# Preparing two more chunks of a Mish MLP without TensorE transposes, in a fused long-convolution and MLP kernel

## The chip, the cores and the metric

The kernel runs on one core of one Trainium2 chip. The metric is the device time of one execution in microseconds (us). Three runs of the kernel before gave 358.87 us as the median (358.83 to 359.21).

## The reference, cut to what matters

There are S = 2048 positions of D = 448 channels, and an inner width F = 1792. One sum of three terms is computed from q, k, v and x:

```python
xn = layernorm(q)                                  # per position, over D
kv = shift_conv4(k) * v                            # 4-tap causal convolution, per channel
y  = irfft(rfft(kv, 2S) * rfft(ssm_k, 2S))[:S] + kv * ssm_D
h  = xn @ w1 + b1
out = q + xn * y + mish(h) @ w2                    # mish(h) = h * tanh(softplus(h))
```

## The kernel before

**The MLP.** The 2048 positions are cut into 8 chunks of 256 (two halves, jj = 0 and 1, of 128). A chunk goes through 7 pairs of F tiles, so there are 56 pairs, and the work is written out in slots: slot 2i is GEMM 1 of pair i (22 matmuls of 256 columns, L512), slot 2i+1 holds the Mish of pair i (ScalarE, L520), its split into a high and a low part (a cast on ScalarE, a subtraction on VectorE, L84 and L85) and GEMM 2 of pair i-2 (12 matmuls of 448 columns, L544 to L546). Chunk c owns slots 14c to 14c+13. Both GEMMs are made of products of high and low parts, to keep float32 precision. When a chunk's last pair is through, its PSUM is added to q and so evicted (g2_evac, L551) on VectorE, at slot 2(7c+9): slot 18 for chunk 0, slot 32 for chunk 1. The store of the result is issued on SyncE one slot later (g2_out, L557), except for the last two chunks.

**The convolution** runs between. A "visit" is one group of matmuls (f1_mm, L146) of the first FFT step, over two row blocks: 8 visits of the filter h, at the slots of H_AT (L26), and 8 of kv, at those of KV_AT (L27: 24, 29, 34, 39, 44, 50, 55, 59). Below, h5 or k1 is the load of that visit's tensor (h_load L132, k_load L172, v_load L176). Before a kv visit, VectorE makes the four taps (taps, L189 to L202); the third tap's product is made on GpSimd (taps_pool, L182), started by a memset on VectorE (L181) that stands directly ahead of a fold. Behind a visit comes the fold (f1_fold): ScalarE copies one PSUM half to SBUF (L152), VectorE adds and subtracts (L156). Both write the tile `st`, of which there are two in turn; f1_out stores it to DRAM (L167), for kv from ScalarE's queue three slots after the visit. From slot 66 on, the later FFT steps follow.

**Getting x into GEMM 1.** GEMM 1 needs the normalised chunk with channels on partitions, as XH (high) and XL (low). There are two ways, and NT (4 before) is the first chunk that takes the second.

- Chunks 0 to 3: q is loaded with positions on partitions (ln_load, L390), its mean and spread are taken (bn_stats L406, bn_aggr L409, eps L412 on VectorE, the power on GpSimd L415), GpSimd subtracts and multiplies (norm, L419; tail, L423), TensorE transposes four 128x128 blocks for each half into a PSUM tile of GEMM 1's pool (L464), and the result is copied to XH (ScalarE, L476) and subtracted to XL (VectorE, L474). For chunk 2 this stands at slots 14 to 26, for chunk 3 at 28 to 40.
- Chunks 4 to 7: the host hands in q transposed as well, and xT_load (L434, 512 KB) reads a chunk of it into the one tile XN. The same statistics are taken; mean and reciprocal spread are stored to a small DRAM tile MR by a GpSimd DMA (nt_store, L442); nt_row (L445) reads them back for one half, broadcast to all 128 partitions, into `idr`; nt_norm (L451) subtracts and multiplies with that row, two VectorE operations over 512 elements for each half; nt_split copies to XH (ScalarE, L458) and subtracts to XL (VectorE, L459).

`idr` lies over the identity matrix that the transposes use, and there is one of it: the row of the second half waits until the first half is normalised.

**Order.** Nothing is reordered: each engine executes its instructions in program order, and each DMA is issued from the queue of its engine, in its order, after the waits it carries. `at(slot, ...)` puts work ahead of a slot's Mish and matmuls, `after(slot, ...)` behind them. Small VectorE steps of the statistics go into a list, `drip`, one of which is issued at each `dv()`; "flush" issues what is left. The slots for chunks from NT on are given relative to a base, b:

```python
NT_AT = {"q": -5, "x": -1, "stats": -2, "flush": 0, "row": (4, 8), "norm": (7, 10), "split": (8, 11)}
NT_SOON = dict(NT_AT, row=(4, 5), norm=(4, 7), split=(6, 8))
```

The weights w1 and w2 are loaded and split into high and low parts in the first 15 slots (w2_split, L84 and L85); w2's pair 5 is split behind slot 13 and used in slot 15.

Of the kernel before, what the change touches and what calls it, by code (L numbers as in the profile page):

```python
# [17 lines left out]
NP = NF // 2  # L18
CH = 256
NCHUNK = S // CH  # L20
NO = 8
EPS = 1e-5

G2_LAG = 2
# [5 lines left out]
I2_AT = {100: ((6, 7, 0, 1), 92, (95, 97, 98, 99), (0, 2, 0, 1)),  # L30
         108: ((2, 3, 4, 5), 101, (104, 105, 106, 107), (0, 1, 0, 1))}
LATE = 2
NT = 4
NT_AT = {"q": -5, "x": -1, "stats": -2, "flush": 0, "row": (4, 8), "norm": (7, 10), "split": (8, 11)}
NT_SOON = dict(NT_AT, row=(4, 5), norm=(4, 7), split=(6, 8))
NT_HOW = {c: NT_SOON for c in (3, 4, 7)}
NT_HOW[5] = dict(NT_AT, q=-8, stats=-4, flush=-2)
WARM_N = (448, 448, 448)
FILL_N = (224, 112, 96)
# [3 lines left out]
def tile_kernel(ctx: ExitStack, tc, q, qT, k, v, sk, hT, sD, w10, w1, w2, c_fib, c_g, c_gi, c_i2, out):  # L43
    nc = tc.nc
    V = nc.vector
# [17 lines left out]
    Dkv = dp.tile([NO * 16, 32, D], F32, name="Dkv")  # L63
    E = dp.tile([NJ * 4, 64, D], F32, name="E")
    MR = {c: dp.tile([2, CH], F32, name="MR") for c in range(NT, NCHUNK)}

# [8 lines left out]
    def rs(c):  # L75
        return rstd[:, 2 * c:2 * c + 2] if c < NT else mv[:, 2 * c:2 * c + 2, 1]

# [26 lines left out]
    def dv(n=1):  # L104
        for _ in range(n):
            if drip:
                drip.pop(0)()
# [4 lines left out]
    def at(slot, fn, *args):  # L112
        plan.setdefault(int(slot), []).append((fn, args))

    def after(slot, fn, *args):
        plan2.setdefault(int(slot), []).append((fn, args))
# [278 lines left out]
    def xn_tile():  # L395
        return mp.tile([128, 4, CH], F32, name="xn", bufs=1)

    def ln_parts(c):
        st = mp.tile([128, 2, 6], F32, name="bst", bufs=2)
        ve = mp.tile([128, 2], F32, name="ve", bufs=2)  # L400
        if c < NT:
            XN[c] = xn = xn_tile().rearrange("p a b -> p (a b)").rearrange("p (j d) -> p j d", j=2)
        eng = nc.gpsimd if 0 < c < NCHUNK - 1 else V

        def stats(jj):
            V.bn_stats(st[:, jj], Q[c][:, jj])  # L406

        def aggr(jj):
            V.bn_aggr(mv[:, 2 * c + jj], st[:, jj])  # L409

        def eps(a, b):
            V.tensor_scalar(ve[:, a:b], mv[:, 2 * c + a:2 * c + b, 1], EPS, None, op0=ALU.add)  # L412

        def power(a, b):
            nc.gpsimd.tensor_tensor(rs(c)[:, a:b], ve[:, a:b], mhalf[:, a:b], op=ALU.pow)  # L415

        def norm(jj):
            j = 2 * c + jj
            eng.tensor_scalar(xn[:, jj, :D], Q[c][:, jj], mv[:, j, 0:1], rs(c)[:, jj:jj + 1],  # L419
                              op0=ALU.subtract, op1=ALU.mult)  # L420

        def tail(a, b, copy=eng.tensor_copy):
            copy(xn[:, a:b, D:], xn[:, a:b, D - 64:D])  # L423

        return stats, aggr, eps, power, norm, tail, ve
# [21 lines left out]
    def nt_norm(c, jj):  # L447
        x = XN[c][:, :, 128 * jj:128 * jj + 128]
        for t, op in enumerate((ALU.subtract, ALU.mult)):
            m = idr.rearrange("p (a t) -> p t a", t=2)[:, t:t + 1].to_broadcast([128, 4, 128])  # L450
            V.tensor_tensor(x, x, m, op=op)  # L451
            dv()

    def nt_split(c, jj):
        if jj == 0:
# [22 lines left out]
    def ln_T(c, jj):  # L478
        if jj == 0:
            dv(len(drip))  # L480
            x_tiles(c)
        p = pg()
        transposes(c, jj, p)
        for lo in range(2):
            x_split(c, jj, p, lo)
# [73 lines left out]
    def mlp_slot(s):  # L559
# [3 lines left out]
        if half == 0:  # L563
            if i < n:
                c, p = pairs[i]
                if c + 1 < NT:
                    if p == 0:
# [8 lines left out]
        else:  # L576
            if i < n:
                c, p = pairs[i]
                if p == NP - 2 and c + 1 < NT:
                    ln_T(c + 1, 0)  # L580
# [27 lines left out]
    for g, t in enumerate(KV_AT):  # L608
        d = t - (KV_AT[g - 1] if g else t - 6)
        at(t - d - (3 if g > 1 else 2), k_load, g)  # L610
        at(t - d - 1, v_load, g)
        for u in range(4):
            after(t - (2 if g else 1) - d + d * u / 4, taps, g, u)
        at(t, f1_mm, KV, g, "kv")
        if g + 1 < NO:
            after(t, taps_pool, g + 1, 2)
        after(t, f1_fold, g, "kv")
        at(t + (3 if g < NO - 1 else 2), f1_out, Dkv, g, "kv")

    for p in range(NP):  # L620
        if p >= 3:
            at(max(2 * p - 5, 0), w1_load, p)
        if p == 1 or p > 2:
            at(2 * p - 2, w1_split, p)
        p and at(2 * p + (1 if p < 5 else 0), w2_load, p)
        at(2, w2_split, p) if p == 0 else after(2 * (p + G2_LAG) - 1, w2_split, p)

    at(OCT_AT[0], regroup)
    for o in range(NO):
# [34 lines left out]

    for c in range(NT, NCHUNK):
        at_ = NT_HOW.get(c, NT_AT)
        b = 2 * NP * (c - 1) + (1 if c == NT else 0)
        at(b + at_["q"], ln_load, c)
        at(b + at_["x"], xT_load, c)
        at(b + at_["stats"], nt_stats, c)  # L670
        at(b + at_["flush"], lambda: dv(len(drip)))
        for jj in range(2):
            at(b + at_["row"][jj], nt_row, c, jj)
            after(b + at_["norm"][jj], nt_norm, c, jj)
            after(b + at_["split"][jj], nt_split, c, jj)
# [28 lines left out]
    stats, aggr, eps, power, norm, tail, ve = ln_parts(0)  # L704
# [120 lines left out]
```

## Time and profile before

| what | value |
|---|---|
| median of three runs | 358.87 us |
| the profiled execution's own time | 359.38 us |
| its span in the trace | 357.6 us |
| busy time of TensorE (PE) | 352.0 us |
| busy time of VectorE (DVE) | 269.1 us |
| busy time of ScalarE (ACT) | 156.8 us |
| busy time of GpSimd (POOL) | 76.5 us |
| transposes, L464, 32 of them | 5.0 us |
| GpSimd's normalising, L419, 6 of them | 15.8 us |

The profile is of one execution. Its span runs from the first to the last instruction; the execution's own time is 1.8 us longer. PE is TensorE's matmul, PEld its weight load, and a Q behind an engine's name (SPq, ACTq) is that engine's queue of DMA issues. A row of a timeline gives the start, the duration, the engine, the line, the operation and what it writes and reads, and in square brackets the idle time ahead of it and what ended it. A row of the chain of waits gives the start, the time that it holds in the chain, the engine, the tile and the line. A row of waits gives who waited for whom: us in all, times, longest. Durations of neighbouring rows on TensorE overlap, since matmuls are pipelined, so 5.0 us of transposes is not 5.0 us of the span.

### The profile page before, as it was taken

Reading aid. Unit: us, or ns where it says so; the run is one execution under the profiler, and the core shown is the slowest. Engines: PE = TensorE matmul, PEld = TensorE weight load, DVE = VectorE, ACT = ScalarE, POOL = GpSimd, SP = SyncE. Lnnn points to the kernel's source line nnn. Section 1 sums busy time; section 2 is a strip of 40 time slices with the busy share of each in tenths; the row PEclk is TensorE's granted clock in tenths of the full one; section 3 lists DMA queues with packets and bytes.
Section 4 is the critical chain, followed back from the end, with each engine's and each line's share of the span. In section 5 each row is a group of like instructions: output and inputs, shape, how many; then the busy total and the mean of one; then the engine's idle time right before and its main releaser. Section 6 shows DMA issues by size and latency. Waiting matters only on the chain.

```text
span 357.6 us, 7445 instructions
## 1 busy us (share of the span) xinstructions
PE 352.0 (98%) x3100; PEld 290.2 (81%) x3100; DVE 269.1 (75%) x371; ACT 156.8 (44%) x267; POOL 76.5 (21%) x81
## 2 busy tenths in 40 slices
PE   8999999999999999999999999999999999999995
PEld 2988888888888989889997758767775699979795
DVE  5999568999999899899537757756863933788942
ACT  3976643344241542342333453455445343354480
POOL 2037001920128240213000030011031116040030
PEclk9999999999999999999999999999999999999999
DMA  7999978849586446763869569999994386989176
GB/s 242 353 373 303 408 291 221 242 124 285 145 262 217 148 120 169 222 162 82 250 208 353 203 175 295 241 279 310 284 260 131 81 240 252 408 316 284 32 113 144
DMA packets 30227, 82.48 MB, mean 231 GB/s; under 512 B 3057, under 2 KB 15474, under 8 KB 30194
## 3 DMA queue, kind: packets, MB, share of 16 engines
q1 hardware_dynamic: 21410, 47.03, 39.2%
q0 software_dynamic: 4896, 22.95, 22.8%
q10 hardware_dynamic: 3888, 12.03, 12.4%
q8 instruction: 24, 0.39, 0.5%
q14 instruction: 9, 0.07, 0.1%
HBM read 53.55 MB, written 28.45 MB: 229 GB/s over the span
## 4 chain that ended last, share of the span: by engine, by line
PE 86%; DMA 5%; DVE 3%; issue 3%; POOL 2%; SPq 0%; ACT 0%; ACTq 0%; POOLq 0%
PE pg L512 18%; PE pg L544 12%; PE pg L546 12%; PE pg L545 11%; PE pq L512 7%; PE pp L512 5%; PE pr L512 4%; PE pq L146 3%; DMA Dh<-st 3%; PE pp L235 3%; PE pr L235 3%; PE pp L274 2%; DMA kr<-in_w_dram 2%; PE pq L235 2%; PE pr L274 1%
## 5 line engine op out<-in xcount | busy, mean ns | idle before, releaser
L544 PE MATMUL pg<-w2h,ach 128*128 128x448 f32 x224 | 82.4, 368 | 0.0
L545 PE MATMUL pg<-w2l,ach 128*128 128x448 f32 x224 | 81.3, 363 | 0.2 <-DVE w2l L85 0.2
L546 PE MATMUL pg<-w2h,acl 128*128 128x448 f32 x224 | 81.4, 363 | 0.0
L85 DVE TENSOR_TENSOR acl<-a,ach 128x512 fp32r<-128x512 f32 x56 | 38.9, 695 | 32.1 <-ACT ach L84 32.0
L520 ACT ACTIVATE a<-pg,b1t 128x256 f32<-128x256 f32 x66 | 27.8, 472 | 64.3 <-PE pg L512 57.5
L512 PE MATMUL pg<-XH,w1h 128*128 128x256 f32 x264 | 52.7, 283 | 0.0
L544 PEld LDWEIGHTS pg<-w2h,ach 128*128 128x128 f32 x224 | 41.9, 187 | 10.8 <-issue 6.4
L512 PEld LDWEIGHTS pg<-XH,w1h 128*128 128x128 f32 x264 | 41.3, 188 | 6.8 <-issue 6.3
L545 PEld LDWEIGHTS pg<-w2l,ach 128*128 128x128 f32 x224 | 42.1, 188 | 2.9 <-DVE w2l L85 0.5
L546 PEld LDWEIGHTS pg<-w2h,acl 128*128 128x128 f32 x224 | 42.0, 188 | 2.4
L512 PE MATMUL pg<-XL,w1h 128*128 128x256 f32 x264 | 42.9, 277 | 0.0
L156 DVE TENSOR_TENSOR st<-pq,st 128x896 f32<-128x896 f32 x32 | 34.8, 1089 | 5.7 <-ACT st L152 5.0
L512 PEld LDWEIGHTS pg<-XL,w1h 128*128 128x128 f32 x264 | 35.9, 188 | 0.0
L84 ACT CAST ach<-a 128x512 fp32r<-128x512 f32 x56 | 34.8, 622 | 1.7
L512 PE MATMUL pg<-XH,w1l 128*128 128x256 f32 x198 | 33.5, 278 | 0.0
L182 POOL TENSOR_TENSOR x<-kr,skb 128x896 f32<-128x896 f32 x8 | 17.0, 2126 | 71.8 <-DVE x L181 58.6
L512 PEld LDWEIGHTS pg<-XH,w1l 128*128 128x128 f32 x198 | 27.6, 188 | 0.0
L199 DVE TENSOR_TENSOR x<-x 128x896 f32<-128x896 f32 x24 | 26.4, 1100 | 1.0 <-POOL x L182 0.3
L520 ACT ACTIVATE a<-pq,b1t 128x256 f32<-128x256 f32 x20 | 8.4, 471 | 31.8 <-PE pq L512 31.8
L285 POOL DMA_DIRECT2D E<-qe x14 | 8.7, 629 | 63.0 <-ACT qe L282 63.0
L152 ACT COPY st<-pr 128x896 f32<-128x896 f32 x16 | 14.5, 907 | 14.8 <-PE pr L146 12.4
L415 POOL TENSOR_TENSOR mv<-ve,mhalf 128x2 f32<-128x2 f32 x4 | 3.9, 986 | 62.8 <-DVE ve L412 62.8
(138 smaller groups left out, 612.8 us busy)
## 6 DMA issues: line engine op xcount, KB each, us to landing
Dkv<-st ACTq DMA_DIRECT2D x16, 448.0 KB, 6.0
ah<-Dh SPq DMA_DIRECT2D x8, 896.0 KB, 7.7
av<-Dkv SPq DMA_DIRECT2D x8, 896.0 KB, 8.6
e<-E POOLq DMA_DIRECT2D x8, 896.0 KB, 7.4
E<-qe POOLq DMA_DIRECT2D x14, 448.0 KB, 5.9
kr<-in_k_dram SPq DMA_DIRECT2D x10, 448.0 KB, 7.0
Dh<-st ACTq DMA_DIRECT2D x10, 448.0 KB, 6.3
x<-in_hT_dram SPq DMA_DIRECT2D x8, 448.0 KB, 6.8
```

Source lines behind the costliest of these rows:

```text
L84: nc.scalar.copy(h, raw)
L85: V.tensor_sub(l, raw, h)
L152: nc.scalar.copy(st[:, 1], o)
L156: f(st[:, n], e, st[:, 1])
L182: nc.gpsimd.tensor_mul(o, KR[g - u // 2], skb[:, u:u + 1].to_broadcast([128, 2, D]))
L199: V.tensor_add(KV[g], KV[g], o)
L235: nc.tensor.matmul(p[32 * t:32 * t + 32, r, :D], g[rs, t, c], a[rs, t], start=True, stop=True, tile_position=(64 * r, 32 * t))
L512: nc.tensor.matmul(ps[n], l, r, start=all(m[0] != n for m in seq[:n_]), stop=all(m[0] != n for m in seq[n_ + 1:]))
L520: nc.scalar.activation(a[:, n], ps[n], AF.Mish, bias=b1t[:, 2 * p + n:2 * p + n + 1])
L544: nc.tensor.matmul(ps, ah[:, n, cs], w2h[:, f], start=f == 0, stop=False)
L545: nc.tensor.matmul(ps, ah[:, n, cs], w2l[:, f], start=False, stop=False)
L546: nc.tensor.matmul(ps, al[:, n, cs], w2h[:, f], start=False, stop=f == NF - 1)
```

## The change

NT goes from 4 to 2, so chunks 2 and 3 take the second way: their 16 transposes, GpSimd's norm and tail and the copies out of PSUM go, and each has a load of the transposed chunk, a store of MR, two row loads, four multiplies or subtractions and two splits. For these two chunks (NORM_POOL) the subtraction and multiplication with the row run on GpSimd and not on VectorE. Their slots come from the base (15 for chunk 2, 29 for chunk 3):

| step | chunk 2 before | chunk 2 after | chunk 3 before | chunk 3 after |
|---|---|---|---|---|
| load q | 14 | 10 | 28 | 20 |
| load transposed q | none | 14 | none | 28 |
| statistics, from | 18 | 13 | 34 | 26 |
| statistics, flushed | 25 | 15 | 39 | 27 |
| rows | none | 19, 20 | none | 33, 34 |
| norm (behind the slot) | with the statistics | 19, 22 | with the statistics | 33, 36 |
| split | 25, 26 | 21, 23 | 39, 40 | 35, 37 |

GEMM 1 first needs chunk 2 at slot 28 and chunk 3 at slot 42. Below, norm(2,0) is the normalising of chunk 2's first half, row (2,1) the row load of its second. The bases of chunks 4 to 7 stay as they were.

Two further edits: the stores of the kv visits at even slots (visits 0, 2, 4 and 5, at slots 24, 34, 44 and 50) are issued behind the Mish of their slot and not ahead of it, and the split of w2's pair 5 is made ahead of slot 12's matmuls and not behind slot 13.

```diff
-NT = 4
+NT = 2
...
-NT_HOW = {c: NT_SOON for c in (3, 4, 7)}
+NT_HOW = {c: NT_SOON for c in (4, 7)}
+NT_HOW[2] = NT_SOON
+NT_HOW[3] = dict(NT_SOON, q=-9, stats=-3, flush=-2)
+NORM_POOL = 2, 3
...
-            V.tensor_tensor(x, x, m, op=op)
-            dv()
+            (nc.gpsimd if c in NORM_POOL else V).tensor_tensor(x, x, m, op=op)
+            c in NORM_POOL or dv()
...
-        at(t + (3 if g < NO - 1 else 2), f1_out, Dkv, g, "kv")
+        (at if t % 2 else after)(t + (3 if g < NO - 1 else 2), f1_out, Dkv, g, "kv")
...
-        at(2, w2_split, p) if p == 0 else after(2 * (p + G2_LAG) - 1, w2_split, p)
+        if p in (0, 5):
+            at(2 if p == 0 else 12, w2_split, p)
+        else:
+            after(2 * (p + G2_LAG) - 1, w2_split, p)
...
-        b = 2 * NP * (c - 1) + (1 if c == NT else 0)
+        b = 2 * NP * (c - 1) + (1 if c < 5 else 0)
```

## The prediction

> **What bounds the kernel now.** I read the page first: the shares, then the chain that ended last, then what TensorE waits for.
>
> ```profile
> span 357.6 us, 7445 instructions
> PE 352.0 (98%) x3100; PEld 290.2 (81%) x3100; DVE 269.1 (75%) x371; ACT 156.8 (44%) x267; POOL 76.5 (21%) x81
> ...
> PE pg L689 <- DVE wz L685: 1.0, 1, 1.0
> PE pq L146 <- DMA x<-in_hT_dram: 0.6, 1, 0.6
> PE pg L545 <- DVE w2l L85: 0.2, 1, 0.2
> ```
>
> TensorE is busy in 352.0 of 357.6 us, and its three waits add up to 1.8 us. So work taken off TensorE comes off the end one for one, and a wait put onto it is added one for one. The table by stretches (window; busy us and instructions of PE, PEld, DVE, ACT, POOL; clock; DMA share; GB/s) shows which engine comes next:
>
> ```profile
> 0.00:51.00 51.00, 49.08 (x366) 38.70 (x366) 38.91 (x62) 32.73 (x52) 12.64 (x19) 1.00 0.95 344
> ...
> 63.00:97.00 34.00, 34.00 (x269) 29.30 (x268) 33.36 (x44) 13.28 (x24) 11.94 (x8) 1.00 0.69 195
> 97.00:113.00 16.00, 16.00 (x121) 14.57 (x121) 15.86 (x24) 5.29 (x10) 6.87 (x5) 1.00 0.87 287
> ```
>
> From 63 to 113 us VectorE is as full as TensorE (33.36 of 34, 15.86 of 16), and chunks 2 and 3 are prepared just there. Whatever delays VectorE before a deadline of TensorE there can become a wait of TensorE.
>
> **The transposes** stand in four groups of four. A group overlaps its neighbours, so I price it by whole stretches of the chain of waits, with and without it:
>
> ```profile
> 71.85 2.72 PE pg L512 x22
> 74.57 0.44 PE pg L464 x4
> 83.96 2.52 PE pg L512 x22
> 95.02 0.52 PE pq L146 x2
> 95.96 2.72 PE pg L512 x22
> 101.08 0.52 PE pq L146 x2
> 107.14 2.51 PE pg L512 x22
> 112.04 2.51 PE pg L512 x22
> 123.83 2.51 PE pg L512 x22
> ```
>
> From 71.85 to 83.96 lie GEMM 1, transposes, GEMM 2, a visit's matmuls, transposes, GEMM 1, GEMM 2: 12.11 us. The same without transposes lies from 95.96 to 107.14: 11.18 us. So chunk 2's two groups cost 0.93 us. For chunk 3, 112.04 to 123.83 is 11.79 us, against 11.06 us from 83.96 to 95.02: 0.73 us. **Removed: 1.66 us.** The PSUM tile that they borrowed from GEMM 1 comes free too, worth nothing, since no wait of GEMM 1 for it is listed.
>
> **The split of w2's pair 5** goes from behind slot 13 ahead of slot 12. Its late end is the 0.2 us wait of L545 above.
>
> ```profile
> 28.40 0.42 SPq L379 DMA_DIRECT2D x<-in_w_dram  x1
> x<-in_w_dram SPq DMA_DIRECT2D x1, 448.0 KB, 5.8
> 38.73 0.59 ACT L476 CAST XH<-pg 128x512 fp32r<-128x512 f32 x1 [1.12 <-PE pg L464]
> ```
>
> The raw tile lands by 34.6. ScalarE stood idle for 1.12 us before 38.73, and the copy fits into that. **Removed: 0.2 us;** it costs nothing unless the tile lands over 3 us later, in which case the split of chunk 1 would wait behind it.
>
> **The new loads early on.** The query row block of chunk 2 is loaded four slots sooner and its transposed block (512 KB) is new. SyncE issues that one only when chunk 1's transposes are done, about 38.7, so the loads behind it (h5, k0, v0) go out 3 us later. The engines move 344 GB/s there, so 512 KB are 1.5 us. The first user, the first tap of visit 0, stands behind slot 17, in the stretch after 51 us, ten us and more behind the issue. I cost it at nothing, and at up to 1 us if the loads land late in the full stretch (0.95). Chunk 2's statistics move from the crowded stretch to slots 13 to 15, where VectorE has gaps (38.91 busy of 51); behind them VectorE would wait for a visit's matmuls anyway, so I count nothing for it.
>
> **The row and the normalising of chunk 2** hang on a chain of their own: statistics, the store of mean and reciprocal spread to DRAM, the row back to all partitions, GpSimd's two multiplies, the copy and the split. The two landing lines are those of the MR store (L442) and of the row load (L445).
>
> ```profile
> 47.76 0.69 DVE L85 TENSOR_TENSOR acl<-a,ach 128x512 fp32r<-128x512 f32 x1 [1.32 <-ACT ach L84]
> ...
> DMA to landing us min/median/max: 3.4/3.9/6.6
> ...
> DMA to landing us min/median/max: 3.7/5.0/9.7
> ...
> L182 POOL TENSOR_TENSOR x<-kr,skb 128x896 f32<-128x896 f32 x8 | 17.0, 2126 | 71.8 <-DVE x L181 58.6
> ...
> 61.00 2.12 POOL L182 TENSOR_TENSOR x<-kr,skb 128x896 f32<-128x896 f32 x1 [26.77 <-DVE x L181]
> ...
> 64.07 1.10 DVE L199 TENSOR_TENSOR x<-x 128x896 f32<-128x896 f32 x1
> ```
>
> VectorE was done with slot 13's work at 46.44 (47.76 less 1.32), the split of w2 in it; so chunk 2's statistics are out by about 47, and power and issue on GpSimd end near 49 (about 1 us each, an estimate). The store lands near 53, the row near 58 by the medians, 56 to 65 by the ends. No trace shows GpSimd's multiply with the strided row. Its nearest row, L182, is 2126 ns for 896 elements, so 1.2 us for 512: norm(2,0), two of them, would end at 60.6, or 61.8 with half as much again for the stride and for VectorE beside it. I take 61.8; below 60.6 nothing is gained. Behind it on GpSimd stands the third tap of visit 0, which starts at 61.00 today: it would start at 61.8 and end at 63.9, just before VectorE adds it (L199 at 64.07 today). So up to here it is just hidden, and every us more goes into VectorE's queue.
>
> **SyncE behind that row.** norm(2,0) also releases the second row (2,1), which is next in SyncE's queue; behind it stand the load of q for chunk 3, moved ahead to slot 20 (its buffer waits for chunk 0's store), h6, k1 and v1.
>
> ```profile
> 56.98 0.35 SPq L557 DMA_DIRECT2D out_dram<-qt  x1
> 58.67 1.08 SPq L172 DMA_DIRECT2D kr<-in_k_dram  x1
> ...
> kr<-in_k_dram SPq DMA_DIRECT2D x10, 448.0 KB, 7.0
> ...
> DMA to landing us min/median/max: 4.4/5.9/9.9
> ...
> 69.86 1.08 DVE L189 TENSOR_TENSOR x<-kr,skb 128x896 f32<-128x896 f32 x1
> ```
>
> Chunk 0's store goes out at 56.98 and needs 4.4 us at the least (the landing line is that of L557), so q goes out at about 62 (by the median 63), h6 and k1 each about half a us after it. k1 leaves at about 63.3 instead of 58.67 and lands at 70.3 by its median of 7.0, where VectorE wants it at 69.86 (L189). **A lateness of about half a us,** 0 to 1.5; what is hidden behind 4.6 us of slack today is hidden no longer.
>
> **VectorE up to chunk 1's eviction.** This is the deadline with the least room: GEMM 2 of chunk 2 needs the PSUM that the eviction (L551) empties.
>
> ```profile
> 96.07 1.15 DVE L551 TENSOR_TENSOR qt<-pg,qt 128x448 f32<-128x448 f32 x2
> 98.51 0.36 PE L544 MATMUL pg<-w2h,ach 128*128 128x448 f32 x1
> ...
> L406 DVE BATCH_NORM_STATS2 bst<-qt 128x6 f32<-128x448 f32 x16 | 9.6, 618 | 2.7 <-DMA qt<-in_q_dram 2.7
> ...
> 67.37 2.78 POOL L419 TENSOR_SCALAR xn<-qt,mv,rstd 128x448 f32<-128x448 f32 x1
> 68.45 1.49 DVE L202 TENSOR_TENSOR x<-x 128x896 f32<-128x896 f32 x1
> 80.60 1.09 DVE L202 TENSOR_TENSOR x<-x 128x896 f32<-128x896 f32 x1
> ```
>
> The first half of the eviction ends near 96.65 and TensorE wants it at 98.51: 1.86 us of room today. TensorE comes 1.13 us sooner (0.93 + 0.2). Chunk 3's statistics (behind the eviction today, slot 34) come ahead of it, to slots 26 and 27: two of 618 ns, partly overlapped, and three short ones, 1.4 us. Chunk 2's two splits stay ahead of it either way. Given back: about 0.3 us (VectorE follows TensorE's 0.2 us; eps of chunk 2 is out of the way) and 0 to 0.8 us where GpSimd's tensor_scalar slowed VectorE (L202 took 1.49 us beside it and 1.09 us without), as far as the multiplies do not do the same; I take 0.3. So 1.86 - 1.13 - 1.4 + 0.3 + 0.3 = -0.07: the room is used up. The late k1 and the late tap then come through in full: **TensorE waits about 0.7 us** (0.5 for k1, 0.2 for the rest), 0 at best, 2 to 3 with both late. The visit's matmuls at 101.08 have the same room (their PSUM is freed behind the same queue) and add nothing. Behind that VectorE is rid of those statistics and catches up, so chunk 3's 0.73 us are kept.
>
> **The stores behind the Mish.**
>
> ```profile
> 81.58 0.84 ACT L520 ACTIVATE a<-pg,b1t 128x256 f32<-128x256 f32 x2 [1.20 <-PE pg L512]
> 87.91 0.91 ACT L152 COPY st<-pr 128x896 f32<-128x896 f32 x1
> Dkv<-st ACTq DMA_DIRECT2D x16, 448.0 KB, 6.0
> ```
>
> Of the four only visit 0's store has a near successor: visit 1's copy (L152, 87.91) takes the same buffer. Today it is issued ahead of the Mish of 81.58; behind that and its cast it goes out by 83.5, lands at 89.5, and the copy comes 1.6 us later than 87.91. VectorE arrives there about then as well, by the late statistics; cost 0, at most 1 us. No row shows a Mish held up by these stores, so the gain is nothing too.
>
> **Sum:** 1.66 + 0.2 - 0.7 = 1.16 us. From the profiled execution, 359.38 us (span 357.6 and 1.8 around it), that is 358.2; the median of the runs shown is 358.87, 0.5 lower, so I predict **357.7 us**.
>
> **One rule against the change.** The Trainium skill, GPSIMD Engine Reference, section 1 (Specifications), says that GpSimd shares its SBUF interface with VectorE and is in contention with VectorE instructions that have two SBUF inputs. The L202 pair above agrees. By that rule norm(2,1), which falls between taps, would slow both engines; it is a reason for the third rival.
>
> **The rivals.**
> 1. *Full gain*: k1 and the tap arrive in time, VectorE keeps pace. 358.87 - 1.86 = 357.0. For it: the medians miss by only half a us. Against: 33.36 of 34 us are busy.
> 2. *The wait eats the gain*: TensorE waits 1.2 to 2.5 us at visit 1's copy, the eviction or the visits, 358.2 to 359.5. For it: the room is -0.07 before any lateness.
> 3. *Slower: GpSimd's norm(2,0) ends late* (a late row, or multiplies as slow as L419, whose 2.78 us for 448 elements would be 3.2 us for each 512). Its price is its end less 61.8, since the third tap, row (2,1) and k1 all hang behind it, on top of 0.2 us. It turns into a loss from an end at 63.5; with the row at its worst landing (65) it ends near 68, and the time would be about 363. At an end of 65.3 I get 360.7. For it: two such multiplies from 58 end at 64.4; against: L182's rate gives 60.6, and L182 is a multiply of the same kind.
> 4. *It does not do what it says*: the transposes were hidden. The stretches speak against it; chance under 1 in 50, put with rival 2.
>
> **How the numbers follow.** Forecast 0.38 (357.3 to 358.1), rival 1 0.22, rival 2 (with 4) 0.20, rival 3 0.20. A measurement of this kernel tells about 0.2%, 0.7 us, from no change. So faster is 0.60, same 0.20, slower 0.20. The range goes from full gain with 0.2 us to spare, 356.8, to 359.8; beyond it lies most of rival 3.
>
> **What would show it.** No L464 beyond chunk 1's; the stretches of 12.11 and 11.79 us shorter by 0.93 and 0.73. The wait of L545 for w2l gone. In 85 to 101 us a wait of TensorE for L551, L156 or L85: its sum is my 0.7. The row (2,1) issue right after norm(2,0), k1 out at 63 to 64, and VectorE idle before L189 of visit 1. I am wrong if TensorE waits elsewhere, for instance in chunk 4, or if norm(2,0) takes over 4 us.

## The result and the profile after

| | before | after |
|---|---|---|
| median | 359.04 us (358.83 to 359.47, 4 runs) | 362.10 us (361.57 to 364.24, 4 runs) |
| the profiled execution | 359.38 us, span 357.6 | 361.66 us, span 359.6 |

The ratio after to before is 1.0099, 95% interval 1.0078 to 1.0121: the kernel became 1% slower. The forecast was 357.7 us, and the range ended at 359.8.

From the changed file's line 40 or so on, its numbers are three higher than before: the visit's matmuls are L149, the copy L155, the fold L159, the third tap on GpSimd L185, VectorE's taps L192 to L205 (L205 is the product with v), the split L88, the row load L448, the two operations with the row L454. In the experiments they move by a few more.

First the page of the kernel after: the span, then busy time, share and instructions of each engine.

```profile
span 359.6 us, 7426 instructions
...
PE 351.4 (98%) x3084; PEld 289.0 (80%) x3084; DVE 272.5 (76%) x371; ACT 157.1 (44%) x267; POOL 75.2 (21%) x83
```

The 16 transposes are gone (3084 matmuls, 3100 before). But VectorE is busy 3.4 us *longer* than before, 272.5 against 269.1, with just as many instructions, 371. Nothing was given to it: the operations with the row run on GpSimd. So some of the same instructions became longer. Next, TensorE's waits in the kernel after (who waited for whom: us, times, longest):

```profile
PE pq L149 <- DVE x L205: 1.7, 1, 1.7
PE pq L149 <- DVE st L159: 1.1, 1, 1.1
PE pg L695 <- DVE wz L691: 1.0, 1, 1.0
PE pg L547 <- DVE qt L554: 0.3, 1, 0.3
PE pq L149 <- DMA x<-in_hT_dram: 0.2, 1, 0.2
```

The wait for w2 went, as said. Two are new, 1.7 and 1.1 us, and neither stands in the stretch from 85 to 101 us where I looked for my 0.7. TensorE's timeline of the kernel after (start, duration, operation, in brackets the idle time ahead and its cause) says where they are:

```profile
72.10 0.59 PE L149 MATMUL pq<-x,con 32*64 32x448 f32 x2 [1.71 <-DVE x L205]
...
79.46 0.59 PE L149 MATMUL pq<-x,con 32*64 32x448 f32 x2 [1.14 <-DVE st L159]
```

The first is kv visit 0 itself, which waits for its taps; the second is h6, behind it, which waits until the fold of visit 0 has emptied the PSUM. The starts of the visits on TensorE show how the difference grows and shrinks (read from the two timelines, us):

| visit | before | after | later by | what lies between |
|---|---|---|---|---|
| h5 | 59.88 | 59.36 | -0.52 | w2's wait gone (h4 is 0.52 sooner already) |
| kv 0 | 70.84 | 72.10 | +1.26 | wait of 1.71 for the taps |
| h6 | 77.36 | 79.46 | +2.10 | wait of 1.14, one group of transposes less |
| kv 1 | 86.41 | 88.19 | +1.78 | one group less |
| kv 2 | 101.01 | 103.10 | +2.09 | late eviction of chunk 1 |
| kv 4 | 128.67 | 130.03 | +1.36 | chunk 3's two groups less |
| kv 5 | 144.54 | 146.46 | +1.92 | late eviction of chunk 2 |

From kv 1 to kv 2 no wait is listed; there GEMM 2 of chunk 2 starts at 100.45 us, right behind the first half of a late eviction (99.77 on VectorE, 96.07 before). Behind kv 5 the distance stays at 1.9 us. So the transposes do pay: from kv 2 to kv 4 it falls by 0.73, the very figure of the prediction. What was wrong is what stands against it.

Now VectorE's timeline of the kernel after, from the fold ahead of visit 0 to the first tap of visit 1, and once more around chunk 3's second half:

```profile
61.41 2.22 DVE L159 TENSOR_TENSOR st<-pq,st 128x896 f32<-128x896 f32 x2 [2.13 <-ACT st L155]
64.79 1.09 DVE L202 TENSOR_TENSOR x<-x 128x896 f32<-128x896 f32 x1 [1.16 <-POOL x L185]
65.80 1.82 DVE L88 TENSOR_TENSOR acl<-a,ach 128x512 fp32r<-128x512 f32 x1
67.54 1.73 DVE L195 TENSOR_TENSOR x<-kr,skb 128x448 f32<-128x448 f32 x1
69.19 0.61 DVE L197 TENSOR_TENSOR x<-kr,skb 128x448 f32<-128x448 f32 x1
...
70.96 1.09 DVE L205 TENSOR_TENSOR x<-x 128x896 f32<-128x896 f32 x1
...
72.77 1.09 DVE L192 TENSOR_TENSOR x<-kr,skb 128x896 f32<-128x896 f32 x1
...
100.84 2.20 DVE L159 TENSOR_TENSOR st<-pq,st 128x896 f32<-128x896 f32 x2
...
109.11 2.18 DVE L202 TENSOR_TENSOR x<-x 128x896 f32<-128x896 f32 x1
111.21 1.79 DVE L88 TENSOR_TENSOR acl<-a,ach 128x512 fp32r<-128x512 f32 x1
```

and GpSimd's in the same stretches:

```profile
59.98 2.69 POOL L454 TENSOR_TENSOR xn<-xn,con 128x512 f32<-128x512 f32 x2 [11.97 <-DMA con<-MR]
62.63 2.13 POOL L185 TENSOR_TENSOR x<-kr,skb 128x896 f32<-128x896 f32 x1
65.76 3.02 POOL L454 TENSOR_TENSOR xn<-xn,con 128x512 f32<-128x512 f32 x2 [1.01 <-DMA con<-MR]
...
99.99 2.69 POOL L454 TENSOR_TENSOR xn<-xn,con 128x512 f32<-128x512 f32 x2 [5.19 <-DMA con<-MR]
...
109.03 3.42 POOL L454 TENSOR_TENSOR xn<-xn,con 128x512 f32<-128x512 f32 x2
```

Lay the two on each other. norm(2,1) runs from 65.76 to 68.78, and the two VectorE operations that start in that time take 1.82 and 1.73 us; the same operations take 0.68 (L88) and 0.61 to 0.62 us (L195, L197) elsewhere. At 109.03 it is the same: 2.18 in place of 1.09, 1.79 in place of 0.68. Each pair of GpSimd operations that falls between taps costs VectorE 2.2 us. The folds at 61.41 and 100.84, which also run beside such a pair but read one of their inputs from PSUM, are not slowed (2.22 and 2.20 us for two).

This gives the first wait. Before, the last product for visit 0 (L205, then L202) ended at 69.94 and TensorE began at 70.84: 0.9 us of room. After, it ended at 72.05, 2.11 later. Of these, 0.72 are the third tap (64.79 against 64.07); the other 1.39 are two operations slowed by 2.24, less some 0.8 by which GpSimd's L419 slowed L202 (1.49, in the prediction) and this split in the kernel before (VectorE's timeline):

```profile
65.17 1.05 DVE L85 TENSOR_TENSOR acl<-a,ach 128x512 fp32r<-128x512 f32 x1
```

TensorE came 0.52 sooner. 2.11 + 0.52 - 0.9 is the wait of 1.7.

SyncE's queue of the kernel after (DMA issues) shows the part that the prediction had seen:

```profile
55.25 0.33 SPq L448 DMA_DIRECT2D con<-MR  x1
...
62.69 0.32 SPq L448 DMA_DIRECT2D con<-MR  x1
63.10 1.34 SPq L393 DMA_DIRECT2D qt<-in_q_dram  x1
64.55 0.37 SPq L135 DMA_DIRECT2D x<-in_hT_dram  x1
64.97 0.44 SPq L175 DMA_DIRECT2D kr<-in_k_dram  x1
```

k1 goes out at 64.97, 6.3 us later than before. Yet VectorE does not wait for it (no idle time ahead of 72.77): it arrives late enough itself. Whether that load costs anything can't be read from this trace.

### The profile page after: what moved, and what is told of

Read it like the earlier page. It is cut to its first block, busy times and chain, and to the rows that moved or that the text cites. A ratio compares the mean times of both kernels' runs of the same rounds, so it can differ in the third digit from the quotient of the medians.

```text
span 359.6 us, 7426 instructions
## 1 busy us (share of the span) xinstructions
PE 351.4 (98%) x3084; PEld 289.0 (80%) x3084; DVE 272.5 (76%) x371; ACT 157.1 (44%) x267; POOL 75.2 (21%) x83
## 4 chain that ended last, share of the span: by engine, by line
PE 77%; DVE 13%; DMA 3%; issue 3%; POOL 2%; ACT 0%; SPq 0%; DVEq 0%; POOLq 0%
PE pg L515 15%; PE pg L547 10%; PE pg L549 10%; PE pg L548 10%; PE pq L515 7%; PE pp L515 5%; PE pr L515 4%; DMA x<-in_hT_dram 3%; DVE x L202 3%; PE pp L238 3%; PE pr L238 3%; PE pq L149 3%; POOL x L185 2%; DVE acl L88 2%; PE pp L277 2%
## 5 line engine op out<-in xcount | busy, mean ns | idle before, releaser
L88 DVE TENSOR_TENSOR acl<-a,ach 128x512 fp32r<-128x512 f32 x56 | 40.8, 728 | 31.4 <-ACT ach L87 30.7
L159 DVE TENSOR_TENSOR st<-pq,st 128x896 f32<-128x896 f32 x32 | 34.8, 1088 | 5.3 <-ACT st L155 4.6
L202 DVE TENSOR_TENSOR x<-x 128x896 f32<-128x896 f32 x24 | 27.3, 1137 | 2.7 <-POOL x L185 1.6
L185 POOL TENSOR_TENSOR x<-kr,skb 128x896 f32<-128x896 f32 x8 | 17.0, 2128 | 38.8 <-issue 21.2
L418 POOL TENSOR_TENSOR mv<-ve,mhalf 128x2 f32<-128x2 f32 x6 | 5.4, 897 | 82.8 <-DVE ve L415 82.8
L155 ACT COPY st<-pr 128x896 f32<-128x896 f32 x16 | 14.5, 906 | 18.5 <-PE pr L149 14.9
L288 POOL DMA_DIRECT2D E<-qe x14 | 8.7, 628 | 63.5 <-ACT qe L285 63.4
```

Of the source, the lines that this page charges most:

```text
L88: V.tensor_sub(l, raw, h)
L155: nc.scalar.copy(st[:, 1], o)
L159: f(st[:, n], e, st[:, 1])
L185: nc.gpsimd.tensor_mul(o, KR[g - u // 2], skb[:, u:u + 1].to_broadcast([128, 2, D]))
L202: V.tensor_add(KV[g], KV[g], o)
```

## The experiments

The theories. **A**: GpSimd's operations with two SBUF inputs hold up VectorE's that have two as well, 2.2 us for each half that falls between taps. **B**: the chain from the row over the first half to the third tap is late, and the second row and k1 behind it. **C**: chunk 3's statistics crowd VectorE ahead of chunk 1's eviction. **D**: the later store of visit 0 holds up a buffer. **E**, formed on the way: k1 is late behind SyncE's wait.

Kernels sent together share the runs of the kernel before, whose medians were 358.94 (e1 to e4), 359.02 (e5 to e8), 358.67 (e9 to e11) and 358.71 us (e12).

| run | what | median, us | ratio to before, 95% |
|---|---|---|---|
| (after) | the change | 362.10 | 1.0078 to 1.0121 |
| e1 | no second half on GpSimd | 362.12 | 1.0059 to 1.0115 |
| e2 | no first half on GpSimd | 360.17 | 1.0024 to 1.0051 |
| e3 | stores back ahead of the Mish | 362.92 | 1.0068 to 1.0120 |
| e4 | before, with the w2 edit alone | 358.80 | 0.9990 to 1.0008 |
| e5 | neither half | 358.64 | 0.9977 to 1.0013 |
| e6 | second half on VectorE | 365.23 | 1.0164 to 1.0196 |
| e7 | both halves on VectorE | 363.23 | 1.0098 to 1.0133 |
| e8 | halves beside folds | 362.80 | 1.0086 to 1.0142 |
| e9 | k1 ahead of the second row | 364.19 | 1.0139 to 1.0167 |
| e10 | e8 and e9 | 358.80 | 0.9989 to 1.0007 |
| e11 | e5 and e9 | 357.38 | 0.9952 to 0.9977 |
| e12 | one large input on GpSimd | 363.43 | 1.0123 to 1.0165 |

**e1: no second half.**

```diff
 def nt_norm(c, jj):
+    if c in NORM_POOL and jj == 1:
+        return
```

> The changed kernel without GpSimd's subtraction and multiplication for the second halves of chunks 2 and 3, which leaves those halves unnormalised. Theory A (GpSimd's two-input operations hold up VectorE's operations with two SBUF inputs; 2.3 us of VectorE at 65 to 69 us and 2.2 us at 109 to 113 us): the cast subtraction beside it is back from 1.82 to 0.7 us, the wait of TensorE for kv visit 0 (1.7 us) goes, that ahead of filter visit 6 shrinks below 0.5 us, and the time is about 359.2 us. Theory B (the chain row, first half, third tap, second row, k1 is late): nothing of that chain changes up to the third tap, so the waits stay and the time is 361.5 us or more. Theory C (chunk 3's statistics crowd VectorE ahead of chunk 1's eviction): 361.5 us or more as well.

362.12 us in the median: no better than the change, where A had said 359.2. The trace does not refute A. The wait of visit 0 is gone in it, as A said, and h6 waits for 0.55 us. But in that execution the row of the first half came a us sooner, and the first half, harmless in the kernel after beside a fold, now fell between two taps. GpSimd's and then VectorE's timeline of e1:

```profile
58.97 3.42 POOL L456 TENSOR_TENSOR xn<-xn,con 128x512 f32<-128x512 f32 x2 [11.98 <-DMA con<-MR]
```

```profile
59.04 2.18 DVE L202 TENSOR_TENSOR x<-x 128x896 f32<-128x896 f32 x1
61.14 1.80 DVE L88 TENSOR_TENSOR acl<-a,ach 128x512 fp32r<-128x512 f32 x1
```

The same slowing, 1.09 and 1.11 us, at another place. I put the rest of the median down to lower clocks (last section): the one execution of e1 with a mean clock of 1.00 took 360.42, and the three at 0.994 to 0.995 took 361.94 to 363.61. The two of the changed kernel that had no such dip took 361.6.

**e2: no first half.** The same edit with `jj == 0`.

> The changed kernel without GpSimd's subtraction and multiplication for the first halves of chunks 2 and 3, which leaves those halves unnormalised. Theory B: the third tap of visit 0 is no longer late (VectorE waited 1.16 us for it) and the second row and k1 come some 3 us sooner, so the wait for kv visit 0 goes and the time falls to about 359.5 us. Theory A: the second half still runs beside the taps, so some 2 us of VectorE are still lost at each place and only the late tap's 0.8 us is won: about 361.2 us.

360.17, between the two. The third tap is on time again, which B said; the second half still slows L88 and L195 (1.70 and 1.73 us), which A said. Each has its part.

**e3: stores back ahead of the Mish.**

```diff
-        (at if t % 2 else after)(t + (3 if g < NO - 1 else 2), f1_out, Dkv, g, "kv")
+        at(t + (3 if g < NO - 1 else 2), f1_out, Dkv, g, "kv")
```

> The changed kernel with the four kv stores issued ahead of the Mish again. Theory D (the later store of visit 0 holds the copy of visit 1 and through it VectorE): the copy comes sooner and the time falls by 0.5 us or more, to 361.5 us or less. Theories A, B and C: no change beyond 0.3 us, about 362 us.

362.92, nothing gained in the median. That alone does not settle D: the one execution with a mean clock of 1.00 took 361.08, half a us less than the two of the change without a dip. The trace of the change says more: there the copy behind visit 1 ends at 91.31 us (ScalarE, L155, 90.40 + 0.91), and VectorE's fold behind it (L159, 92.35) has no idle time ahead of it. The late store of visit 0 held up nothing there, so D has no place to act in that execution.

**e4: the w2 edit alone** (the last but one block of the change's diff) in the kernel before.

> The kernel before with nothing but the split of w2's pair 5 moved ahead of slot 12. All theories: the wait for that split goes. In the two traces TensorE reached filter visit 4 at 48.39 in place of 48.91 us, of which 0.06 us was there already at slot 15; so 0.46 us less, 358.6 us, where the prediction had 0.2 us, 358.8 us.

358.80, ratio 0.9999. In the trace w2's wait is gone and the stretch that held it (45.95 to 48.91 before, 46.36 to 48.86 in e4) is 0.46 us shorter; in the time nothing is seen. In e4's trace the part ahead of it, from the first visit to 46.36 us, is 1.05 us longer than before (38.72 against 37.67); in the kernel after, which has the same edit, it is 37.67 as before, so the edit alone does not cause that. Why nothing is left in the median stays open.

**e5: neither half.** The edit of e1 without the condition on jj.

> The changed kernel without GpSimd's subtraction and multiplication for chunks 2 and 3 altogether, which leaves both chunks unnormalised; loads, rows, statistics and splits stay. If GpSimd's multiplies are the whole loss, by what they hold up on VectorE (theory A) and by the third tap behind them (theory B) together, the waits of TensorE at visits 0 and 6 go, the runs lie within 1 us of each other, and the time is 357.6 to 358.4 us, below the kernel before. Theory C (the statistics of chunk 3 ahead of chunk 1's eviction, the new loads and rows): 359.5 us or more, with waits of TensorE between 85 and 105 us.

358.64: 3.5 us less than the change, the same as before the change, and above the 357.6 to 358.4 that was expected. The ten executions lie 3.4 us apart (357.41 to 360.81), not within 1 us. VectorE's timeline of e5, then TensorE's waits:

```profile
63.14 1.08 DVE L202 TENSOR_TENSOR x<-x 128x896 f32<-128x896 f32 x1
64.24 0.69 DVE L88 TENSOR_TENSOR acl<-a,ach 128x512 fp32r<-128x512 f32 x1
64.85 0.62 DVE L195 TENSOR_TENSOR x<-kr,skb 128x448 f32<-128x448 f32 x1
...
67.16 1.09 DVE L205 TENSOR_TENSOR x<-x 128x896 f32<-128x896 f32 x1
...
71.14 1.09 DVE L192 TENSOR_TENSOR x<-kr,skb 128x896 f32<-128x896 f32 x1 [2.29 <-DMA kr<-in_k_dram]
```

```profile
PE pq L149 <- DVE st L159: 1.8, 1, 1.8
```

VectorE is done with visit 0's taps at 68.25, 3.8 us sooner than in the kernel after, and now stands 2.29 us before the first tap of visit 1: k1 isn't there. The fold of visit 0 stands behind those taps in VectorE's order, and so h6 waits 1.8 us. What the kernel after hid, this one shows: E.

**e6 and e7: on VectorE.** e6 gives VectorE the second half, e7 both (`NORM_POOL = ()`).

> The changed kernel with the second halves of chunks 2 and 3 normalised on VectorE and the first halves on GpSimd. Theory A: a second half then costs VectorE its two operations, 1.4 us, in place of the 2.2 us that GpSimd's take from it, so 0.8 us less at each place, visit 0 waits about 1 us and the time is about 361 us. If GpSimd's multiplies cost VectorE less than 1.4 us, the time rises, to 362.5 us or more.

> The changed kernel with all four halves normalised on VectorE. Theory A: 1.4 us of VectorE for each half in place of 2.2 us, and the third tap no longer stands behind a multiply; but VectorE now waits itself for chunk 2's first row, which landed at 60 us, where it had 2.1 us to spare. About 360.5 us. Theory B alone: the tap is on time and the time falls to 359.5 us.

365.23 and 363.23 us. VectorE waits 2.75 us (e6) and 3.39 us (e7) for k1, and h6 waits 5.2 and 4.4 us for the fold. They say little on A, which the expectation of e6 had asked; they put the weight on E.

**e8: beside folds.** GpSimd's halves are moved to where VectorE reads PSUM: the third tap of visit 0 goes first on GpSimd, those of visits 1 and 3 move as well, norm(2,1) and norm(3,0) are started by a one-element VectorE operation ahead of a fold, norm(3,1) runs on VectorE; the splits and one DMA issue of GpSimd's move to fit.

```diff
+BESIDE = {(2, 1): 24, (3, 0): 34}
...
+        if (c, jj) in BESIDE:
+            y = XN[c][0:1, 0, 128 * jj:128 * jj + 1]
+            V.tensor_scalar(y, y, 0.0, None, op0=ALU.add)
...
+    for (c, jj), t in BESIDE.items():
+        plan2[t].insert(0, (nt_norm, (c, jj)))
```

> A version built on theory A: GpSimd's operations are put where VectorE reads PSUM or is idle. The third tap of visit 0 starts beside the fold of filter visit 4, that of visit 1 at slot 18, that of visit 3 beside the fold of filter visit 7; norm(2,1) is held by a one-element VectorE operation until the fold of visit 0, norm(3,0) until that of visit 2; norm(3,1) runs on VectorE. Theory A: no VectorE operation over 1.3 us between 60 and 115 us but one or two, waits of TensorE below 1 us, 357.8 to 358.8 us. Theories B and C: the row, the loads and the statistics are as before, so 360.5 us or more.

362.80. The slowing is mostly gone (L203 takes 1.30 us ahead of visit 0, 1.63 and 1.75 us behind the folds of visits 0 and 2, in place of 1.09), and again the time did not follow. VectorE's timeline and TensorE's waits of e8 (L193 is the first tap here):

```profile
73.01 1.09 DVE L193 TENSOR_TENSOR x<-kr,skb 128x896 f32<-128x896 f32 x1 [3.90 <-issue]
```

```profile
PE pq L150 <- DVE st L160: 2.9, 1, 2.9
```

VectorE arrives at 69.1 and gets k1 at 73.0 (the profile finds no releaser here; the instruction's only new input is k1, issued at 65.23). My expectation had left E out.

**e9: k1 ahead of the second row.** The row (2,1) is issued two slots later, behind h6 and k1, and chunk 3's q goes back to slot 24.

```diff
-NT_HOW[2] = NT_SOON
-NT_HOW[3] = dict(NT_SOON, q=-9, stats=-3, flush=-2)
+NT_HOW[2] = dict(NT_SOON, row=(4, 7))
+NT_HOW[3] = dict(NT_SOON, q=-5, stats=-3, flush=-2)
```

> The changed kernel with SyncE's queue mended and nothing else: chunk 2's second row is issued behind k1 (slot 22 in place of 20), and q of chunk 3 at slot 24 in place of 20. Theory E (k1, queued behind the row that waits for GpSimd and behind q, whose buffer waits for chunk 0's store, lands at 71 to 74 us where VectorE wants it by 68 to 70): k1 is issued near 58 us and VectorE waits for it nowhere; the wait of TensorE ahead of filter visit 6 goes. But GpSimd's multiplies still take 2.2 us from VectorE ahead of visit 0, so about 1.7 us of waiting stay there: about 360.5 us. If theory E alone is the loss: 358.5 us or less. If theory A alone: 362 us as before.

364.19, 2 us *slower* than the change. k1 goes out at 58.40 and nobody waits for it. But in this run the first half ended at 63.67 and the second began at 67.63, nearer to the deadline. VectorE's timeline of e9, and TensorE's waits:

```profile
65.78 1.09 DVE L202 TENSOR_TENSOR x<-x 128x896 f32<-128x896 f32 x1 [2.40 <-POOL x L185]
...
67.93 1.73 DVE L197 TENSOR_TENSOR x<-kr,skb 128x448 f32<-128x448 f32 x1
69.69 2.06 DVE L202 TENSOR_TENSOR x<-x 128x896 f32<-128x896 f32 x1
```

```profile
PE pq L149 <- DVE x L205: 4.3, 2, 2.8
```

2.40 us of waiting for the third tap, 2.1 us of slowing, and visit 0 waits 2.8 us: A and B undiminished, with E taken away. The second wait in that row, 1.6 us, is visit 3's, where chunk 3's second half (3.92 us from 111.58) runs beside two operations of VectorE (1.81 and 1.73 us). All four executions had a mean clock of 0.993 or 0.994.

**e10: e8 with e9's queue.**

> Both remedies: GpSimd's operations beside folds and gaps as in the run before, and SyncE's queue mended as in the run of that name. If the two are the whole loss: k1 on time, no VectorE operation over 1.7 us between 63 and 110 us, waits of TensorE below 1 us in all behind 60 us, and 357.3 to 358.2 us, faster than the kernel before. If something else holds (statistics, the stores): 359 us or more.

358.80: 5.4 us better than e9, which has the same queue, but outside the 357.3 to 358.2 that was expected and below the 359 of its rival. TensorE's waits and VectorE's timeline of e10:

```profile
PE pg L551 <- DVE qt L558: 0.6, 1, 0.6
```

```profile
64.49 1.78 DVE L203 TENSOR_TENSOR x<-x 128x896 f32<-128x896 f32 x1
```

The waits of visit 0 and h6 are gone. Three operations slowed by 0.6 to 0.7 us are left (this one, and L203 of 1.68 us at 76.70 and 1.75 us at 107.27), each where GpSimd's 2.7 us reach past the end of the fold's 2.2. A wait for chunk 1's eviction is left as well: from h7 to kv 2 e10 takes 6.95 us (94.43 to 101.38), against 6.06 before and in e11. So the deadline that the prediction named costs 0.9 us here.

**e11: e5 with e9's queue.**

> SyncE's queue mended and no multiplies of GpSimd for chunks 2 and 3, which leaves both unnormalised: the bound of what the change can bring with neither loss. 1.66 us of transposes and up to 0.5 us of the split less than the kernel before, with a small wait for the eviction: 357.0 to 357.6 us, against 358.6 us with the queue as the change has it.

357.38, ratio 0.9965 (0.9952 to 0.9977): a hit. k1 is there (L192 at 68.81, no wait), and no visit waits. This is what the transposes are worth if nothing is asked of GpSimd in their place: a bound.

e5, e9, e11 and the change make a square:

| | SyncE's order of the change | k1 ahead of the second row |
|---|---|---|
| GpSimd's operations as in the change | 362.10 | 364.19 |
| without them | 358.64 | 357.38 |

The operations cost 3.5 us in one column and 6.8 in the other. The queue costs 1.3 us in the lower row and less than nothing in the upper. Late taps and a late k1 stand one behind the other on VectorE: whoever is later hides the other, and the costs are not to be added. That explains why the queue's 1.3 us vanish in the upper row, but not why e9 is 2.1 us slower than the change. Three things stand beside that in its trace: the first half began a us later (60.97 against 59.98), visit 3 waits, and the clock falls behind visit 0's wait (last section). Which of them the new queue brings about is open.

**e12: one large input on GpSimd.** Is it the length of GpSimd's access or its second input?

```diff
-            (nc.gpsimd if c in NORM_POOL else V).tensor_tensor(x, x, m, op=op)
+            if c in NORM_POOL:
+                nc.gpsimd.tensor_scalar(x, x, idr[:, t:t + 1], None, op0=op)
+                continue
+            V.tensor_tensor(x, x, m, op=op)
```

> The kernel after the change, with GpSimd's subtraction and multiplication by the broadcast row replaced by ones that read one large SBUF input only (a tensor_scalar whose second operand is one number for each partition, taken from the same tile, so that the waits stay as they are). This leaves out the normalising by each position's own mean and spread for chunks 2 and 3. Nothing else moves. Theory A in its strict form (only a GpSimd instruction with two SBUF inputs holds up VectorE's two-input instructions) expects VectorE's operations beside the second half's pair at their own durations (0.6 to 1.1 us in place of 1.7 to 1.8) and a time of 358.6 to 360. The rival, that any GpSimd access to SBUF of that length does it, expects VectorE's operations beside it still at 1.4 to 2.2 us and a time of 361 to 363. A third outcome: GpSimd's operation with one input takes clearly longer than 1.3 us for 512 elements, so that the third tap comes later; then the durations beside it decide, not the time.

363.43 us, by the third outcome: GpSimd took longer. Its timeline in e12, and VectorE's beside the second of them:

```profile
61.00 3.23 POOL L455 TENSOR_SCALAR xn<-xn,con 128x512 f32<-128x512 f32 x2 [12.57 <-DMA con<-MR]
...
68.14 4.90 POOL L455 TENSOR_SCALAR xn<-xn,con 128x512 f32<-128x512 f32 x2 [1.82 <-DMA con<-MR]
```

```profile
68.49 0.62 DVE L197 TENSOR_TENSOR x<-kr,skb 128x448 f32<-128x448 f32 x1
69.15 1.38 DVE L202 TENSOR_TENSOR x<-x 128x896 f32<-128x896 f32 x1
...
71.61 1.09 DVE L465 TENSOR_TENSOR XL<-xn,XH 128x512 fp32r<-128x512 f32 x1
```

Beside 4.9 us of it VectorE loses 0.3 us on L202 and 0.4 on L465 (0.68 elsewhere), nothing on L197, in place of 2.2 beside 3.0 us. Now it is GpSimd that is held up: 2.45 us for each operation, against 1.6 where VectorE mostly stood idle or folded. So with one large input VectorE loses far less, though not nothing; A's strict form, with no loss, is a little too strong. The kind of GpSimd's operation and its pace changed along with the input, so this run does not show that the number of inputs alone decides.

## Why the prediction was wrong

By its own steps:

- **Transposes, 1.66 us: right.** From kv 2 to kv 4 the change gains 0.73. In e11, where no wait covers it, kv 0 to h7 takes 23.17 us (69.95 to 93.12) against 24.11 before (70.84 to 94.95), 0.94 for the predicted 0.93. The 1.3 us by which e11's median beats the kernel before is less than the 1.66; I can't place the rest. The start of the first visit alone differs by 0.66 us between those two traces (7.62 and 8.28).
- **w2's split, 0.2: mis-sized in the trace, 0.5, and not seen in the time** (e4).
- **Early loads and stores at nothing: nothing in the traces speaks against it.** D found no place in the change's trace (e3), and the one wait of TensorE for a load of h, 0.2 us, is shorter than before (0.6).
- **The chain of the row: the mechanism right, the size short.** norm(2,0) was to run from 58.2 to 61.8 and ran from 59.98 to 62.67: its row landed 1.8 us late by my sum, and the two operations took 2.69 us where I had taken 3.6. The third tap ended near 64.8 and not at 63.9, 0.7 us late for VectorE. That the tap was "just hidden" left no us for any of it.
- **k1 late by half a us: mis-sized, and hidden.** Where VectorE came on time it waited 2.29 to 3.9 us (e5 to e8). I had let k1 go out at 63.3; it went out at 64.97 in the kernel after, behind a later row and an issue of q that took 1.34 us.
- **VectorE up to chunk 1's eviction: the step that failed.** Its sum holds "+0.3" for a slowing by GpSimd's tensor_scalar that goes, "as far as the multiplies do not do the same". They did it threefold: 2.24 us around visit 0 against some 0.8 by L419 before, a loss of 1.4 where I booked a gain of 0.3. The rows shown gave a warning and no bound: L202 had 0.4 us of slowing beside an operation with one large input, and I had no row for one with two, so the upper end should have been open. The Trainium skill, GPSIMD Engine Reference, section 1 (Specifications), names VectorE instructions with two SBUF inputs among those that GpSimd contends with; the traces agree, with 1.1 us for each such operation beside a pair of GpSimd's and nothing for folds out of PSUM. I named it "a reason for the third rival" and gave it no price in the sum.
- **The deadline with the least room: wrong.** I named the eviction, with 1.86 us. Visit 0 had 0.9 us (69.94 to 70.84), 0.4 after TensorE's gain, and it comes 28 us earlier (70.84 against 98.51), right behind the late third tap. Chunk 1's eviction came late too: it costs some 0.3 us in the kernel after and 0.9 in e10. C is at most that; no run parts chunk 3's statistics from the slowed operations ahead of it.
- **The rivals.** The third, norm(2,0) late, has the right sign and half the mechanism, but its point was an end at 63.5, and 62.67 lies below that; by its own price, 0.9 us on top of 0.2, it would have left a gain. What made the loss is the sum of its lateness and the slowing of VectorE, and no rival had both.

So 2.1 us were gained (transposes and w2) and about 4 lost in TensorE's waits: 1.8 at visit 0, 1.3 at h6, 0.9 at the evictions of chunks 1 and 2 (from the table of visits: growth of the distance, plus what the group of transposes between had saved). The difference is the 1.9 at which the distance stays. The median is later by 3.1 us; I put the rest down to the executions whose mean clock was 0.994.

Shown: leaving out the operations on GpSimd takes 3.5 us or more off (e5 against the change, e11 against e9); e10's arrangement, with three halves beside folds and one on VectorE, takes most of it back (against e9); mending the queue gains only where those operations are out of the way (the square, and e10 against e8). Only argued: how the 3.5 us divide between the late third tap and the slowing (e1 and e2 show that each has a part), and that the clock (below) makes the rest of the median. No version that does the whole computation beat the kernel before; e10 equals it.

## What to carry to other kernels

Work moved to GpSimd is not free for VectorE: go through VectorE's operations that will run beside it, and price each that reads two tiles in SBUF at its length and 1.1 us more (0.61 became 1.73, 0.68 became 1.82, 1.09 became 2.18, beside GpSimd's operations on 512 elements with two inputs); folds that read PSUM lost nothing here. Check each deadline between the change and the place where you expect the trouble, the nearest first. Where two delays stand one behind the other on an engine, taking one away shows nothing or worse, so test them in a square of four and not one by one.

## What the runs showed of the hardware that I had not expected

A longer wait of TensorE cost its clock as well. Granted clock in the windows of e9 around the wait of 2.8 us ahead of visit 0 (window, length, busy us and instructions of PE, PEld, DVE, ACT, POOL; clock; DMA share; GB/s):

```profile
70.00:73.00 3.00, 0.21 (x9) 0.07 (x11) 2.97 (x3) 0.62 (x1) 0.80 (x1) 1.00 0.75 302
73.00:74.00 1.00, 1.00 (x16) 0.17 (x16) 1.00 (x2) 0.00 (x0) 0.00 (x0) 0.83 0.00 0
74.00:75.00 1.00, 1.00 (x12) 0.97 (x5) 1.00 (x2) 0.84 (x1) 0.00 (x0) 0.50 0.00 0
...
76.00:77.00 1.00, 1.00 (x7) 1.00 (x7) 0.97 (x2) 0.00 (x0) 0.00 (x0) 0.50 0.79 312
```

TensorE works again from 73.0 on, and from about 73.7 to 77 it is granted half its clock: some 1.6 us more, behind a wait of 2.8. The profiled executions of e3 (2.3 us), e12 (2.4), e8 (2.9), e7 (4.4) and e6 (5.2) show the same 3.4 us at 0.50 behind their longest wait; those of the kernel after (1.7), e5 (1.8), e2 (0.9) and e1 (0.6) show none. But the length does not decide alone. In e3 a second wait, of 1.8 us, ahead of visit 3, is followed by such a dip as well (TensorE's timeline, then the windows behind it):

```profile
119.31 0.59 PE L149 MATMUL pq<-x,con 32*64 32x448 f32 x2 [1.77 <-DVE x L205]
```

```profile
120.00:121.00 1.00, 1.00 (x11) 0.71 (x4) 1.00 (x2) 0.58 (x1) 0.00 (x0) 0.94 0.12 27
121.00:122.00 1.00, 1.00 (x4) 0.88 (x3) 1.00 (x3) 0.33 (x1) 0.00 (x0) 0.50 0.00 0
```

In these traces every wait of 2.3 us and more is followed by a dip, none of 1.7 us or less, and of the two of 1.8 us one. What else decides there, the runs do not show. A dip of this size also fits the times: the two executions of the kernel after with a mean clock of 0.997 or more took 361.57 and 361.66 us, the two at 0.994 took 362.54 and 364.24. If it is the same there, which is an inference, since those two have no trace, a wait of some 1.8 us costs its own length in one execution and about 1.6 us more in the next.
